# Two of four weight pieces on a second DMA queue, in a gated mix of linear attention and SwiGLU

## The chip, the cores and the metric

The kernel runs on one core of a Trainium2 chip. The metric is the device time of one execution in microseconds, as the median of several runs; lower is better.

## The reference

The input `x` has 2048 rows (tokens) of 512 values, in bfloat16. Two branches are computed from it and mixed per token. The inputs of branch B called `B_x` are not used; both branches read `A_x`.

```
g = sigmoid((x * gate_w).sum(-1, keepdims=True))
# branch A: linear attention, 32 heads of 16
q, k, v = split(x @ wqkv)
phi(t) = where(t > 0, t + 1, exp(t)) + 1e-6
kv = einsum("bhsd,bhse->bhde", phi(k), v);  z = phi(k).sum over s
a  = (einsum("bhqd,bhde->bhqe", phi(q), kv) / (phi(q) . z + 1e-6)) @ wo
# branch B: SwiGLU with F = 1376
b  = (silu(x @ w1) * (x @ w3)) @ w2
out = g * a + (1 - g) * b
```

## The kernel before

The 2048 tokens are handled in 16 tiles of 128 (`t`), or in 4 blocks of 512 (`tb`). The inner dimension of 512 is split into four chunks of 128 (`kc`). All weights stay in SBUF.

The projections to q and k come first. The weights for both lie in one tile, `wqk` (128 x 4 x 1024); chunk `kc` of it, called piece `kc` below (256 KB), is one load. A projection of one tile of tokens is four matmuls, one for each piece (L183), with the transposed tokens `xT` as the stationary operand. ScalarE (ACT) takes the exponential from PSUM, VectorE (DVE) makes `pk` or `pq` from it, GpSimd (POOL) adds up `pk` for z, and TensorE collects G = x^T phi(k) in four PSUM banks (L231). Then follow, per block, the SwiGLU matmuls (L303 and L309, ten of 128 columns of F each), a remainder of 96 columns together with the gate (L245), the small products that turn G into kv and M2, and the output matmuls (L475 for branch A, L492 for branch B with `w2`), which VectorE mixes (L498) and SyncE stores (L508).

The order of the work is written out by hand: the program runs under a manual schedule, each engine does its instructions in program order, and semaphores join them. Nearly all loads are issued by SyncE (SP, `dq`), in the order of the code. A DMA that SP issues uses one of eight semaphores in turn, and waits for the eighth DMA before it in that count, where that is not known to be over.

The beginning matters here. TensorE first does 13 matmuls on constants (L359). The first two tiles of tokens are loaded as they are (`xN`, L129, one load of 256 KB) and transposed on TensorE with an identity (L365); VectorE (L379, L381, L394) and ScalarE (L380, L382) copy the results to `xT`. The later tiles of `xT` come by transposing loads from SP (`load_xT`, L123), which stand behind the four pieces of `wqk` (`load_wqk`, L126) in SP's queue. The matmuls of the first two tiles are interleaved by piece: four matmuls with piece 0, the transposes for chunk 3, four matmuls with piece 1, and then k alone with pieces 2 and 3, before q with the same pieces:

```python
for kc in range(2):
    for n, t in (("k", 0), ("q", 0), ("k", 1), ("q", 1)):
        first_mm(n, t, kc)
    if kc == 0:
        transpose_kc(3, bank[0])
        nc.vector.tensor_copy(out=xT[:, 3, 0 : 2 * P], in_=bank[0][:, 0 : 2 * P])
for kc in range(2, KC):
    for t in range(2):
        first_mm("k", t, kc)
```

ScalarE begins with a one-column exponential into `act_pre`, a tile that nobody reads, which brings the load of its function table to the front (L130). On its own DMA queue it issues one load, `touch` (L133): 16 columns of pieces 1 to 3, 12 KB, which nobody reads either.

After the x loads SP issues the remainder columns (`wr`), `w1`, `w3`, `wv`, `wo`, `w2` (1.25 MB, one load, L154) and `w2x`.

Of the kernel before, what the change touches and what calls it, by code (L numbers as in the profile page):

```python
# [8 lines left out]
ACT = mybir.ActivationFunctionType  # L9
# [3 lines left out]
BF16 = mybir.dt.bfloat16  # L13
# [3 lines left out]
def kernel(  # L17
# [17 lines left out]
    nc = tc.nc  # L35
    P = nc.NUM_PARTITIONS

    Bb, S, D = A_x.shape
# [3 lines left out]
    KC = D // P  # L42
# [4 lines left out]
    FC = F // P  # L47
# [14 lines left out]
    wqkv_r = A_wqkv.rearrange("(kc d) n -> d kc n", d=P)  # L62
# [3 lines left out]
    consts = ctx.enter_context(tc.tile_pool(name="consts", bufs=1))  # L66
# [5 lines left out]
    warm = nc.const_aps.tensor(1.0, [P, 256], BF16)  # L72
# [7 lines left out]
        out=bmask[:], in_=bmask[:], pattern=[[-Dh, HPC], [0, Dh]], compare_op=ALU.is_ge,  # L80
# [3 lines left out]
        out=bmask[:], in_=bmask[:], pattern=[[Dh, HPC], [0, Dh]], compare_op=ALU.is_ge,  # L84
# [23 lines left out]
    wqk = consts.tile([P, KC, 2 * D], BF16, name="wqk")  # L108
# [6 lines left out]
    w3 = consts.tile([P, KC, F0], BF16, name="w3")  # L115
    w2 = consts.tile([P, FC, D], BF16, name="w2")
    xT = consts.tile([P, KC, S], BF16, name="xT")
    act_pre = consts.tile([P, 1], BF16, name="act_pre")
    dq = nc.sync

    def load_xT(t):
        ts = slice(t * P, (t + 1) * P)
        dq.dma_start(out=xT[:, :, ts], in_=x2d[ts, :], transpose=True)  # L123

    def load_wqk(kc):
        dq.dma_start(out=wqk[:, kc, :], in_=wqkv_r[:, kc, 0 : 2 * D])  # L126

    x_first = x2d[0 : 2 * P, :].rearrange("(p j) d -> p j d", j=2)
    dq.dma_start(out=xN[:, 0:2, :], in_=x_first)  # L129
    nc.scalar.activation(out=act_pre[:], in_=warm[:, 0:1], func=ACT.Exp)  # L130

    touch = consts.tile([P, KC - 1, 16], BF16, name="touch")
    nc.scalar.dma_start(out=touch[:], in_=wqkv_r[:, 1:KC, 0:16])  # L133
    for kc in range(KC):
        load_wqk(kc)
    natural = {3: (2, 4), 5: (4, 8), 8: (8, 16)}
    for t in range(2, NT):
        load_xT(t)
# [3 lines left out]
    with nc.allow_non_contiguous_dma(reason="gate column"):  # L142
        dq.dma_start(
            out=wr[:, :, 2 * FR : NR], in_=gate_w.rearrange("(kc d o) -> d kc o", d=P, o=1)
# [3 lines left out]
    for w, w_r, cuts in ((w1, w1_r, (0, KC)), (w3, w3_r, (0, KC))):  # L148
# [2 lines left out]
    dq.dma_start(out=wv[:], in_=wqkv_r[:, :, 2 * D : 3 * D])  # L151
    dq.dma_start(out=wo[:], in_=A_wo.rearrange("(kc d) n -> d kc n", d=P))
    w2_r = B_w2[0:F0, :].rearrange("(fc f) d -> f fc d", f=P)
    dq.dma_start(out=w2[:], in_=w2_r)  # L154
    w2x_r = B_w2[F0:F, :].rearrange("(i r) d -> i (r d)", i=RP)
    dq.dma_start(
        out=w2x[:].rearrange("p r d -> p (r d)"),
        in_=w2x_r[None].to_broadcast([TPB, RP, RG * D]),
# [442 lines left out]
```

## Time and profile before

| | us |
|---|---|
| median of 3 runs | 178.73 (178.44 to 178.74) |
| the profiled execution, its own time | 177.74 |
| its span in the profile | 176.0 |
| TensorE busy in the span | 171.3 |
| VectorE, ScalarE, GpSimd busy | 110.5, 59.1, 63.3 |

All times in the profile count from the start of the span. The granted clock of TensorE was 1.0 throughout. The profiled execution spends 1.70 us outside the span, and the median of the runs lies 0.99 us above the profiled execution. "PEld" is TensorE's loading of weights, which overlaps its matmuls; "SPq" and "ACTq" are the instructions with which SP and ACT issue DMAs. The landing of a DMA is counted from its issue to the completion of its semaphore.

### The profile page before, as it was taken

The numbers are of one execution on the slowest core, as the hardware profiler recorded it, in microseconds if no ns is written. First come the engines' busy times: TensorE is split into PE (matmuls) and PEld (weight loads), VectorE is DVE, ScalarE is ACT, GpSimd is POOL, SyncE is SP. The second block draws the span as 40 slices with busy tenths as digits, with TensorE's granted clock in tenths as the row PEclk, the third lists the DMA queues.
The fourth block names the chain that finished last, engine by engine and source line by source line (L and its number), as shares of the span: only waits on it lengthen the run. The fifth ranks groups of instructions, "written<-read, shape, count | busy, mean of one in ns | idle before, by whom it ended". The sixth has DMA issues, their size and how long they took to land.

```text
span 176.0 us, 2668 instructions
## 1 busy us (share of the span) xinstructions
PE 171.3 (97%) x952; PEld 82.4 (47%) x969; DVE 110.5 (63%) x207; ACT 59.1 (34%) x109; POOL 63.3 (36%) x106
## 2 busy tenths in 40 slices
PE   8999999999999999999999999999999999999993
PEld 5444444444456443444444466444444444444453
DVE  0399788888764899777343477853435775344363
ACT  4364544544753533322433101224226122422000
POOL 5087656656300668586300044540000662000000
DMA  5988969997205112323200013330000233000001
GB/s 172 277 197 207 164 123 237 403 352 231 78 4 56 22 30 41 78 63 91 58 0 0 0 34 84 84 89 0 0 4 0 60 89 89 4 0 0 30 30 60
DMA packets 29360, 15.58 MB, mean 88 GB/s; under 512 B 21156, under 2 KB 27556, under 8 KB 29348
## 3 DMA queue, kind: packets, MB, share of 16 engines
q1 hardware_dynamic: 28948, 15.41, 35.1%
q8 instruction: 7, 0.11, 0.3%
q10 hardware_dynamic: 400, 0.01, 0.1%
q14 instruction: 5, 0.04, 0.1%
HBM read 8.86 MB, written 2.10 MB: 62 GB/s over the span
## 4 chain that ended last, share of the span: by engine, by line
PE 95%; DMA 2%; issue 1%; SPq 0%; DVE 0%
PE bank L303 20%; PE bank L492 20%; PE bank L309 19%; PE bank L183 16%; PE bank L231 8%; PE bank L475 8%; PE bank L245 3%; DMA wqk<-in_A_wqkv_dram 2%; PE bank L278 2%; PE bank L447 0%; SPq L129 0%; PE bank L462 0%; DVE o L498 0%; PE bank L365 0%
## 5 line engine op out<-in xcount | busy, mean ns | idle before, releaser
L315 DVE TENSOR_TENSOR hT<-bank,sg 128x512 bf16<-128x512 f32 x40 | 27.3, 682 | 31.0 <-PE bank L309 28.9
L303 PE MATMUL bank<-xT,w 128*128 128x512 bf16 x158 | 40.8, 379 | 0.2
L309 PE MATMUL bank<-xT,w 128*128 128x512 bf16 x156 | 40.5, 379 | 0.2
L314 ACT ACTIVATE sg<-bank 128x512 bf16<-128x512 f32 x40 | 23.9, 597 | 45.9 <-PE bank L303 45.9
L492 PE MATMUL bank<-w,hT 128*128 128x512 bf16 (+2 forms) x176 | 37.0, 355 | 0.5 <-issue 0.3
L337 POOL TENSOR_TENSOR pqs<-pq,rden 128x512 bf16<-128x512 bf16 x16 | 16.9, 1057 | 54.3 <-issue 46.8
L183 PE MATMUL bank<-wqk,xT 128*128 128x512 bf16 x126 | 30.2, 379 | 0.1
L215 POOL TENSOR_TENSOR zacc<-zacc,pk 128x128 f32<-128x128 f32 x56 | 23.3, 447 | 10.4 <-DVE pk L201 10.4
L492 PEld LDWEIGHTS <-hT 128*128 128x128 bf16 x180 | 16.7, 98 | 18.4 <-issue 0.8
L309 PEld LDWEIGHTS <-w 128*128 128x128 bf16 x160 | 15.7, 98 | 18.9
L303 PEld LDWEIGHTS <-w 128*128 128x128 bf16 x160 | 15.5, 98 | 18.2 <-issue 0.2
L498 DVE SCALAR_TENSOR_TENSOR o<-bank,omg_all,aga 128x512 bf16<-128x512 f32 (+2 forms) x18 | 12.4, 692 | 14.5 <-PE bank L492 11.7
L183 PEld LDWEIGHTS <-xT 128*128 128x128 bf16 x128 | 12.5, 98 | 14.9 <-issue 0.3
L322 POOL TENSOR_TENSOR pr<-pq,zb 128x512 f32<-128x512 bf16 x16 | 18.4, 1155 | 0.1
L231 PE MATMUL bank<-pk,xN 128*128 128x512 bf16 x62 | 16.3, 379 | 0.2
L475 PE MATMUL bank<-M,pqT 128*128 128x512 bf16 x61 | 15.6, 379 | 0.1
L196 ACT ACTIVATE eq<-bank 128x512 bf16<-128x512 f32 x16 | 9.4, 597 | 16.0 <-PE bank L183 14.9
L201 DVE SCALAR_TENSOR_TENSOR pk<-bank,emk 128x512 bf16<-128x512 f32 x16 | 11.1, 692 | 1.6
L196 ACT ACTIVATE ek<-bank 128x512 bf16<-128x512 f32 x16 | 9.4, 597 | 6.5 <-PE bank L183 6.5
L201 DVE SCALAR_TENSOR_TENSOR pq<-bank,emq 128x512 bf16<-128x512 f32 x16 | 11.1, 692 | 0.5
L326 DVE TENSOR_REDUCE den<-pr 128x32 f32<-128x512 f32 x16 | 10.8, 676 | 0.0
L231 PEld LDWEIGHTS <-xN 128*128 128x128 bf16 x64 | 6.3, 98 | 7.5
(54 smaller groups left out, 95.6 us busy)
## 6 DMA issues: line engine op xcount, KB each, us to landing
w<-in_B_w_dram SPq DMA_DIRECT2D x3, 1280.0 KB, 10.3
out_dram<-o SPq DMA_DIRECT2D x15, 128.0 KB, 1.9
wqk<-in_A_wqkv_dram SPq DMA_DIRECT2D x4, 256.0 KB, 3.7
xN<-in_A_x_dram SPq DMA_DIRECT2D x1, 1024.0 KB
xN<-in_A_x_dram SPq DMA_DIRECT2D x2, 256.0 KB, 2.9
xN<-in_A_x_dram SPq DMA_DIRECT2D x1, 512.0 KB, 4.2
wv<-in_A_wqkv_dram SPq DMA_DIRECT2D x1, 512.0 KB, 11.2
wo<-in_A_wo_dram SPq DMA_DIRECT2D x1, 512.0 KB, 12.2
```

The costliest lines, as they stand in the source:

```text
L183: nc.tensor.matmul(ps[:], lhsT=xT[:, kc, t * P : (t + 1) * P], rhs=w[:, kc, :], start=(kc == 0), stop=(kc == KC - 1),)
L196: nc.scalar.activation(out=e[:], in_=ps[:], func=ACT.Exp)
L201: nc.vector.scalar_tensor_tensor(out=dst, in0=ps[:], scalar=0.0, in1=em[:], op0=ALU.max, op1=ALU.add)
L215: nc.gpsimd.tensor_tensor(out=(zaccb if t == NT - 1 else zacc)[:, cs], in0=zacc[:, cs], in1=pk[t][:, cs], op=ALU.add,)
L231: nc.tensor.matmul(bank[kc][:], lhsT=xN[:, t, kc * P : (kc + 1) * P], rhs=pk[t][:], start=(t == 0), stop=(t == NT - 1),)
L303: nc.tensor.matmul(g_ps[:], lhsT=w1[:, kc, fs], rhs=xT[:, kc, tok], start=(kc == 0), stop=(kc == KC - 1),)
L309: nc.tensor.matmul(u_ps[:], lhsT=w3[:, kc, fs], rhs=xT[:, kc, tok], start=(kc == 0), stop=(kc == KC - 1),)
L314: nc.scalar.activation(out=sg[:], in_=g_ps[:], func=ACT.Silu)
L315: nc.vector.tensor_tensor(out=hT[tb][:, fc, :], in0=u_ps[:], in1=sg[:], op=ALU.mult)
L322: nc.gpsimd.tensor_tensor(out=pr[t][:], in0=pq[:, t, :], in1=zb[:], op=ALU.mult)
L475: nc.tensor.matmul(ps[:], lhsT=pqT[:, c, ts], rhs=M2[:, c, :], start=(c == 0), stop=(c == KC - 1),)
L492: nc.tensor.matmul(ps[:, 0 : cs.stop - cs.start], lhsT=hT[tb][:, fc, tt * P : (tt + 1) * P], rhs=w2[:, fc, cs], start=(fc == 0 and not sta ...
```

## The change

Pieces 1 and 3 of `wqk` are issued by ScalarE instead of SP. The first exponential of ScalarE writes its one column into `wqk[:, 1, 0:1]` instead of `act_pre`, so that the load of piece 1, which overwrites that column, has to wait for it; the load of piece 3 follows on the same queue. The load `touch` is left out. The load of `w2` is split into two halves of five chunks each.

```diff
-    act_pre = consts.tile([P, 1], BF16, name="act_pre")
...
-    def load_wqk(kc):
-        dq.dma_start(out=wqk[:, kc, :], in_=wqkv_r[:, kc, 0 : 2 * D])
+    def load_wqk(kc, queue):
+        queue.dma_start(out=wqk[:, kc, :], in_=wqkv_r[:, kc, 0 : 2 * D])
...
-    nc.scalar.activation(out=act_pre[:], in_=warm[:, 0:1], func=ACT.Exp)
-
-    touch = consts.tile([P, KC - 1, 16], BF16, name="touch")
-    nc.scalar.dma_start(out=touch[:], in_=wqkv_r[:, 1:KC, 0:16])
+    nc.scalar.activation(out=wqk[:, 1, 0:1], in_=warm[:, 0:1], func=ACT.Exp)
+
     for kc in range(KC):
-        load_wqk(kc)
+        load_wqk(kc, nc.scalar if kc in (1, 3) else dq)
...
-    dq.dma_start(out=w2[:], in_=w2_r)
+    for a, b in ((0, FC // 2), (FC // 2, FC)):
+        dq.dma_start(out=w2[:, a:b, :], in_=w2_r[:, a:b, :])
```

## Prediction

> **What bounds the kernel now.** I read the page first (sections 1 and 4), then the chain of waits over the first 9 us, then the timeline of SP's queue, ACT and TensorE there, and last the DMA queues in short windows.
>
> Busy time of the engines and the chain that ended last, from the page:
>
> ```profile
> PE 171.3 (97%) x952; PEld 82.4 (47%) x969; DVE 110.5 (63%) x207; ACT 59.1 (34%) x109; POOL 63.3 (36%) x106
> PE 95%; DMA 2%; issue 1%; SPq 0%; DVE 0%
> ```
>
> TensorE is busy 171.3 of 176.0 us. It begins at 0.84 and the last 2 us are the final store, so some 2 us of idle time can be won anywhere, and the stretches after 9 us show hardly any. The edits all act on loads, so I look where a load still holds TensorE. The chain, first 9 us (start, length, what):
>
> ```profile
> 1.26 3.11 DMA wqk<-in_A_wqkv_dram
> 4.37 0.04 issue
> 4.41 1.02 PE bank L183 x4
> 5.43 0.11 PE bank L365 x2
> 5.54 3.60 PE bank L183 x16
> ```
>
> The first real matmul (L183) starts at 4.41 because piece 0 of wq and wk lands at 4.37. The timeline there (start, length, engine, line):
>
> ```profile
> 0.81 0.39 SPq L129 DMA_DIRECT2D xN<-in_A_x_dram  x1
> 0.86 0.43 ACTq L133 DMA_DIRECT2D touch<-in_A_wqkv_dram  x1
> 1.26 1.84 SPq L126 DMA_DIRECT2D wqk<-in_A_wqkv_dram  x4
> 2.10 0.20 ACT L130 ACTIVATE act_pre<-const-bfloat16-1.0 128x1 bf16<-128x1 bf16 x1
> 4.08 0.28 ACT L380 ACTIVATE xT<-bank 128x128 bf16<-128x128 f32 x1 [1.78 <-PE bank L365]
> 4.32 0.62 PEld L183 LDWEIGHTS <-xT 128*128 128x128 bf16 x4
> 6.83 0.53 PEld L183 LDWEIGHTS <-xT 128*128 128x128 bf16 x3 [0.27 <-issue]
> ```
>
> Two losses stand here. The weights of the first matmul load at 4.32 and it starts 0.09 later; the transposing matmuls (L365) start 0.01 after theirs, at 3.64 and 3.65. So at most 0.08 us hangs on piece 0. And the weight load at 6.83 follows 0.27 us of idleness. The matmul starts there are 6.03, 6.25, 6.46, 6.82, 7.04; the usual spacing is 0.86/4 = 0.216, so one start is 0.14 late, that of the first matmul on piece 3. Issue times and landings, asked piece by piece: piece 0 1.26 + 3.1 = 4.37, piece 1 1.72 + 3.4 = 5.12, piece 2 2.18 + 3.9 = 6.08, piece 3 2.67 + 4.1 = 6.77. TensorE wanted them at 4.33, 5.38, 6.25 and 6.68: piece 3 alone comes late, piece 0 just, and the two between have 0.26 and 0.17 to spare.
>
> The DMA queues (q1 is SP's, q10 ACT's), from 2.0 to 2.9 us, then from 2.9 to 3.3 us, then from 3.3 to 4.0 us; share of 16 engines in the last column:
>
> ```profile
> q1 hardware_dynamic: 105, 0.22, 79.2%
> ...
> q1 hardware_dynamic: 64, 0.10, 66.0%
> q10 hardware_dynamic: 400, 0.01, 56.2%
> ...
> q1 hardware_dynamic: 152, 0.28, 106.8%
> ```
>
> From 2.9 us on the DMA engines are full, so each piece lands when the bytes ahead of it are through. And the small unused load (touch) took its 400 packets all between 2.9 and 3.3: after nearly all of xN (105 packets before 2.9), ahead of piece 0, which SP had issued at 1.26. It cost 56.2% of 0.4 us = 0.22 us of every engine.
>
> **The change, part by part.**
>
> *No touch load.* Everything behind it comes 0.22 us sooner: piece 0 at 4.15, and with the order unchanged piece 1 at 4.90, piece 2 at 5.86, piece 3 at 6.55. Worth 0.08 us at the first matmul, which is then held by its weights. TensorE would want the others at 5.30, 6.17 and 6.60, so piece 3 no longer stalls it: 0.14 us more. Bounds: nothing, if what follows is delayed otherwise; and if xN too comes sooner (its 3.61 sets the transposes), up to 0.2 us more.
>
> *Pieces 1 and 3 on ACT's queue, held by the activation.* The activation does the same 128x1 work and ends at 2.30. Then ACT issues piece 1 and piece 3, 0.43 + 0.03 us each by the touch row: 2.36 to 2.79 and 2.82 to 3.25. Piece 1 goes out 0.64 later than before, piece 3 0.15 later, piece 2 (now second on SP) 0.46 earlier. Behind the waiting instruction on ACT stand only the copies of xT at L380 and L382; L380 starts at 4.08, so 0.83 us of cover is left. If the cover went, each further us would delay the third matmul by as much. No row shows a bulk load on ACT's queue, so its start is bounded: SP's xN was issued at 0.81 and its packets began about 1.92 (1.1 us); touch, the one ACT load, 0.86 and 2.9 (2.0 us). That makes piece 1 ready at 3.47 to 4.4, and piece 3 at 3.9 to 4.9. The last packets of piece 0 leave at about 3.55 to 3.8. I take the near end, because touch's later start is explained by xN having the engines until then. What follows hangs on whose turn it is: touch went ahead of a piece 0 that had been issued 1.6 us earlier, whole and in one go, when xN was through. So I expect piece 0, piece 1 (ACT), piece 2 (SP), piece 3 (ACT), the order of today, and no further cost. The other end is piece 1 behind piece 2, a rival below.
>
> The Trainium skill, "DMA: Bandwidth & Descriptors", section on queues, rings and completion order, says that each DMA engine goes round-robin between queue rows, a whole packet at a time, with some 9 to 17 descriptors in a typical one. The touch rows agree with that turn-taking; whether 2 KB rows keep whole pieces together no run here shows.
>
> *SP two issues shorter.* The transposed loads of xT start at 2.2 instead of 3.15. In the queue they lie behind the same bytes, and nobody waits for them: xT of tile 2 lands at 3.15 + 4.1 = 7.25 and its first matmul is at 8.12. Worth nothing. That they are generated beside ACT's two loads is the third rival.
>
> *w2 in two halves.* One issue of 3.66 us (L154, held back by full queues) becomes two, at most 0.5 us more of SP. SP is free from 36.9 (w2x issued) to 46.1 (the z transpose, for which it waits 9.1 us on POOL), and w2, landing at 43.8, is first read at 67.2. Cost 0; uncovered it would be 0.5. In number, the extra load takes touch's place among the loads that later issues count back to: each issue from z on waits for a load one later in order, none of which lands late (w1 at 33.9, wo at 40.2; zrow is issued at 49.3). Cost 0.
>
> **The sum.** 0.08 + 0.14 = 0.22 us off. The profiled execution took 177.74 us, 1.70 over its span, so 177.52; the median of the runs is 0.99 above it, and taking off the same 0.22 gives 178.5 us. TensorE is dense afterwards, so a shift of the projections moves the end by as much: k of tile 0 is ready for the G products 0.09 before they start (8.89, 8.98), and moves along.
>
> **Rivals.**
>
> *Piece 1 behind piece 2.* If ACT's queue starts by touch's 2.0 us, or the two queues share the engines row by row, pieces 1 and 2 both end where piece 2 would, at 5.86. TensorE waits from 5.30 to 5.86, then runs 4 matmuls (0.86) and 2 (0.43), and takes piece 3 at 7.15 instead of 6.82: +0.33 us, 179.1 us. It decides from the point where piece 1 is ready later than some 3.6. For it: the margin is only 0.1 us. Against it: touch's turn.
>
> The Trainium skill, same page, section on issuing engines, says that loads issued from several engines share the same 16 DMA engines, and only issue time is saved. By that the later issue of piece 1 buys nothing, and it would land with piece 2; the full engines after 2.9 agree.
>
> *ACT's issue held behind SP's transposes.* SP now starts issuing xT (1.30 and 1.26 us each) at 2.23, just before ACT's first issue at 2.36. If both draw on one generator in turn, piece 1 is generated after xT of tile 2, at 3.5, and piece 3 after tile 3, at 4.8. Then L380 waits until 5.2, piece 1 lands about 6.2, TensorE takes 1.29 us for its six matmuls and piece 3 at 7.5: +0.7 us, 179.4 us. Against it: touch's issue (0.43) ran beside xN's (0.39) unslowed; but those were plain loads.
>
> *xN sooner as well.* Touch overlaps xN's tail. If xN came 0.2 us sooner and all else with it: 0.42 off, 178.3 us. Against it: 105 of 128 packets of xN were through before touch began.
>
> **How the numbers follow.** Forecast 0.42, piece 1 late 0.30, held generator 0.16, xN sooner 0.12. A measurement of this kernel tells about 0.2% (0.36 us) from no change. The forecast at 0.22 off lies mostly within that (0.36, and 0.06 faster); the late piece at 0.33 on, with ends of 0.1 and 0.6, splits (0.13 same, 0.17 slower); the held generator is slower (0.16); xN sooner is mostly faster (0.10 and 0.02). Sums: faster 0.16, same 0.51, slower 0.33. The range runs from 178.2, below the last rival, to 179.4, the middle of the third; the forecast's own is 178.35 to 178.75.
>
> **What would show it.** Right: no ACT load of 400 small packets; piece 0's wait gone (first L183 about 0.01 after its weights); no idle weight load before piece 3; the first G product about 0.2 us before 8.98. The late piece: idle TensorE between the transposes of L365 and the fifth L183, some 0.5 us. The held generator: ACT's issues longer than 0.43 us, or L380 later than 4.08. Wrong altogether: a wait after 9 us that is not there now.

## The result, and the profile after

The changed kernel is slower. Its median is 180.19 us (6 runs, 179.60 to 182.39) against 178.58 us for the kernel before on the same chip (6 runs, 177.89 to 178.83); the ratio is 1.0102, 95% interval 1.0081 to 1.0124. The ratio leaves out the run of 182.39 us, in which the granted clock was 0.989 instead of 0.998 to 1.0. The profiled execution took 180.96 us, its span is 179.1 us (before: 177.74 and 176.0).

Busy time of the engines and the chain that ended last, from the page of the changed kernel:

```profile
PE 172.9 (97%) x969; PEld 82.6 (46%) x969; DVE 110.9 (62%) x207; ACT 59.2 (33%) x109; POOL 63.3 (35%) x106
PE 93%; DMA 4%; ACT 1%; ACTq 0%; DVE 0%; issue 0%
```

TensorE's share is unchanged, and the share of the DMAs in the chain has doubled. The chain from 2.1 to 12 us (start, length, what) says where. Line numbers have moved by one to three: L125 loads a piece, L122 an x tile, L181 is the projection, L363 the transposes on TensorE.

```profile
2.10 0.21 ACT wqk L129
2.31 0.02 issue
2.33 0.40 ACTq L125
2.73 0.03 issue
2.76 7.06 DMA wqk<-in_A_wqkv_dram
9.82 0.04 issue
9.86 2.32 PE bank L181 x10
```

The chain no longer runs through piece 0. It runs through ACT: the activation that holds, the issue of piece 1, and piece 3, which takes 7.06 us from its issue to 9.82. The timeline shows the issues and what TensorE did (idle time before in brackets):

```profile
1.25 0.89 SPq L125 DMA_DIRECT2D wqk<-in_A_wqkv_dram  x2
2.19 2.61 SPq L122 DMA_TRANSPOSE xT<-in_A_x_dram  x2
2.33 0.88 ACTq L125 DMA_DIRECT2D wqk<-in_A_wqkv_dram  x2
4.03 0.28 ACT L378 ACTIVATE xT<-bank 128x128 bf16<-128x128 f32 x1 [1.72 <-PE bank L363]
4.29 1.44 PE L181 MATMUL bank<-wqk,xT 128*128 128x512 bf16 x4
7.70 1.45 PE L181 MATMUL bank<-wqk,xT 128*128 128x512 bf16 x6 [1.86 <-DMA wqk<-in_A_wqkv_dram]
9.86 0.38 PE L181 MATMUL bank<-wqk,xT 128*128 128x512 bf16 x1 [0.71 <-DMA wqk<-in_A_wqkv_dram]
```

The first matmul starts at 4.29 instead of 4.41. Then TensorE waits 1.86 us for piece 1, runs six matmuls, and waits again for piece 3. The first matmul on piece 3 stands at 9.86; before it stood at 6.82. That is 3.04 us later, and the span is 179.1 - 176.0 = 3.1 us longer: this execution lost all of it before 10 us. The medians differ by less, 1.6 us; how long the two pieces take differs from execution to execution (piece 3 landed at 9.82 here, and at 9.19 when the same kernel was profiled again).

### The profile page after: what moved, and what is told of

Its sections match the earlier page's. It is cut to its first block, busy times and chain, and to the rows that moved or that the text cites. A ratio compares the mean times of both kernels' runs of the same rounds, so it can differ in the third digit from the quotient of the medians.

```text
span 179.1 us, 2685 instructions
## 1 busy us (share of the span) xinstructions
PE 172.9 (97%) x969; PEld 82.6 (46%) x969; DVE 110.9 (62%) x207; ACT 59.2 (33%) x109; POOL 63.3 (35%) x106
## 4 chain that ended last, share of the span: by engine, by line
PE 93%; DMA 4%; ACT 1%; ACTq 0%; DVE 0%; issue 0%
PE bank L490 19%; PE bank L301 19%; PE bank L307 19%; PE bank L181 14%; PE bank L229 8%; PE bank L473 8%; DMA wqk<-in_A_wqkv_dram 4%; PE bank L243 3%; PE bank L276 2%; ACT L129 1%; PE bank L445 0%; ACTq L125 0%; PE bank L460 0%; DVE o L496 0%; ACT wqk L129 0%
## 5 line engine op out<-in xcount | busy, mean ns | idle before, releaser
L301 PE MATMUL bank<-xT,w 128*128 128x512 bf16 x160 | 41.1, 379 | 0.0
L307 PE MATMUL bank<-xT,w 128*128 128x512 bf16 x160 | 41.1, 379 | 0.0
L490 PE MATMUL bank<-w,hT 128*128 128x512 bf16 (+2 forms) x180 | 37.5, 355 | 0.0
L181 PE MATMUL bank<-wqk,xT 128*128 128x512 bf16 x128 | 31.0, 383 | 2.6 <-DMA wqk<-in_A_wqkv_dram 2.6
L181 PEld LDWEIGHTS <-xT 128*128 128x128 bf16 x128 | 12.5, 98 | 17.9 <-issue 3.5
L473 PE MATMUL bank<-M,pqT 128*128 128x512 bf16 x64 | 16.1, 379 | 0.0
L196 DVE TENSOR_SCALAR emk<-ek 128x512 bf16<-128x512 bf16 x16 | 7.3, 459 | 4.6 <-ACT ek L194 4.6
```

Of the source, the lines that this page charges most:

```text
L181: nc.tensor.matmul(ps[:], lhsT=xT[:, kc, t * P : (t + 1) * P], rhs=w[:, kc, :], start=(kc == 0), stop=(kc == KC - 1),)
L301: nc.tensor.matmul(g_ps[:], lhsT=w1[:, kc, fs], rhs=xT[:, kc, tok], start=(kc == 0), stop=(kc == KC - 1),)
L307: nc.tensor.matmul(u_ps[:], lhsT=w3[:, kc, fs], rhs=xT[:, kc, tok], start=(kc == 0), stop=(kc == KC - 1),)
L473: nc.tensor.matmul(ps[:], lhsT=pqT[:, c, ts], rhs=M2[:, c, :], start=(c == 0), stop=(c == KC - 1),)
L490: nc.tensor.matmul(ps[:, 0 : cs.stop - cs.start], lhsT=hT[tb][:, fc, tt * P : (tt + 1) * P], rhs=w2[:, fc, cs], start=(fc == 0 and not sta ...
```

## The experiments

The table collects what follows: landing of the four pieces in each profiled execution (us from the span's start, good to 0.1 us), the start of the first matmul on piece 3, and the ratio of times to the kernel before with its interval. The first matmul on piece 3 depends on more than the landings: TensorE begins at half its pace, and the moment at which the pace doubles differs between profiles, as shown further down.

| kernel | 0 | 1 | 2 | 3 | matmul on 3 | ratio to before |
|---|---|---|---|---|---|---|
| before | 4.37 | 5.12 | 6.08 | 6.77 | 6.82 | 1 |
| changed | 4.25 | 7.66 | 5.0 | 9.82 | 9.86 | 1.0102 (1.0081 to 1.0124) |
| changed, profiled again | 4.2 | 7.0 | 5.3 | 9.19 | 9.23 | 1.0138 (1.0105 to 1.0172) |
| all pieces on SP | 4.4 | 5.4 | 6.4 | 7.13 | 7.17 | 1.0013 (0.9994 to 1.0031) |
| no hold | 5.51 | 4.5 | 6.6 | 5.9 | 9.77 | 1.0101 (1.0038 to 1.0165) |
| no hold, more warm-up | 5.65 | 4.8 | 6.9 | 6.1 | 8.74 | 1.0054 (1.0038 to 1.0071) |
| x loads plain | 4.25 | 6.84 | 6.6 | 7.6 | 8.18 | 1.0083 (1.0046 to 1.0119) |
| x loads plain, run again | 4.15 | 6.9 | 6.7 | 8.41 | 8.46 | 1.0069 (1.0047 to 1.0092) |
| x loads held back | 4.25 | 6.3 | 5.1 | 6.9 | 7.62 | 1.0177 (1.0147 to 1.0208) |
| only piece 3 on ACT | 4.2 | 6.72 | 7.6 | 7.7 | 8.07 | 1.0052 (1.0018 to 1.0086) |
| one queue, that order | 4.2 | 7.0 | 5.7 | 9.02 | 9.06 | 1.0115 (1.0074 to 1.0156) |
| touch kept | 4.45 | 6.8 | 5.1 | 9.01 | 9.05 | 1.0089 (1.006 to 1.0118) |
| before, w2 in halves | 4.4 | 5.0 | 5.9 | 6.7 | 7.80 | 1.0018 (1.0004 to 1.0032) |

Two theories were set against each other. Theory 1: SP's transposed x loads, now issued 0.9 us sooner, run beside ACT's plain loads on the same DMA engines, and the transposing stalls those. Theory 2: ACT's queue is merely late, and then shares the engines with whatever SP has queued.

**All pieces back on SP.**

```diff
-    nc.scalar.activation(out=wqk[:, 1, 0:1], in_=warm[:, 0:1], func=ACT.Exp)
+    act_pre = consts.tile([P, 1], BF16, name="act_pre")
+    nc.scalar.activation(out=act_pre[:], in_=warm[:, 0:1], func=ACT.Exp)
...
-        load_wqk(kc, nc.scalar if kc in (1, 3) else dq)
+        load_wqk(kc, dq)
```

> Undone: all four pieces back on SP, the first activation writes its own tile again; still without the small unused load and with w2 in halves. If ACT's queue is the cause (both theories below), pieces 1 and 3 land at about 4.9 and 6.6 us and the time is that of before or up to 0.3 us less, 178.3 to 178.6. If the missing small load or the halves of w2 cost the time, it stays near 180.2.

The median was 178.64 us against 178.34 us of before, ratio 1.0013. The loss is gone, so ACT's queue carries it. But nothing was won either: without the small load, pieces 1 to 3 landed 0.3 to 0.4 us later than before, not 0.2 sooner.

**The hold taken away.**

```diff
-    nc.scalar.activation(out=wqk[:, 1, 0:1], in_=warm[:, 0:1], func=ACT.Exp)
+    act_pre = consts.tile([P, 1], BF16, name="act_pre")
+    nc.scalar.activation(out=act_pre[:], in_=warm[:, 0:1], func=ACT.Exp)
```

> The hold alone taken away: ACT issues pieces 1 and 3 from about 0.86 us. Theory 1 (SP's transposed loads beside ACT's plain loads stall both): the pieces are through, all but the end of piece 3, before the first transposed packet at about 5 us, so they land by 5 and 7 us and the time is 178.3 to 179.0; piece 0 may come 0.5 us later, since ACT takes its turn. Theory 2 (ACT's queue is just late, and shares the engines with whatever SP has queued): the same 178.3 to 179.0, if the lateness was the hold; if ACT's queue starts late by itself, piece 1 lands at 6 us or later and the time is 179.5 to 180.2.

A miss: three of four runs took 180.85 to 180.88 us, one 178.85. Pieces 1 and 3 were early, as expected, and cost xN and piece 0 their time. The DMA queues from 2.6 to 3.6 us of this kernel (packets, MB, share of 16 engines):

```profile
q1 hardware_dynamic: 96, 0.19, 49.9%
q10 hardware_dynamic: 66, 0.14, 43.9%
```

ACT's 2 KB packets run mixed with those of xN, 66 beside 96 in the same microsecond. They do not wait until xN is through. TensorE began on x only at 4.29 and got piece 0 at 5.51, and its timeline shows a second loss (L182 is the projection in this kernel, L364 the transposes):

```profile
5.56 1.86 PE L182 MATMUL bank<-wqk,xT 128*128 128x512 bf16 x4 [0.44 <-DMA wqk<-in_A_wqkv_dram]
7.22 0.42 PE L364 MATMUL bank<-ident,xN 128*128 128x128 bf16 x2
7.43 2.93 PE L182 MATMUL bank<-wqk,xT 128*128 128x512 bf16 x8
```

Four matmuls in 1.86 us are some 0.43 us apart; before, four of them took 1.02. The spacing falls to 0.216 only at about 9.5 us. TensorE stood idle for 0.5 us before x and again before piece 0, and kept half its pace for long.

**No hold, but 22 warm-up matmuls.**

```diff
-    warm_step(13)
+    warm_step(22)
```

> The kernel without the hold, with 22 instead of 13 matmuls on constants ahead of the first transposes, so that TensorE does not stand idle while x comes. If TensorE's half pace until 9.4 us was the larger part of that kernel's 180.86 (three of four runs; the fourth 178.85), it now runs at full pace from the first matmul on piece 0 at 5.5 us or soon after, and nearly all runs take 178.6 to 179.3. If the late loads were the cause, it stays at 180.5 to 181.

All ten runs lay between 178.75 and 179.81 us. The median, 179.23, is in the expected range, but five of the ten runs are above it. Full pace came a little later than expected too, about 0.6 us into the matmuls on piece 0, which began at 6.19. The median is 1.6 us below that of the kernel without the longer warm-up, although the warm-up itself holds the first transposes back to 5.5 us. So the half pace was the larger part of the loss in the three slower of the four runs without the hold. (The ratios, 1.0101 and 1.0054, count the fourth run as well, and differ by 0.8 us.) The Trainium skill, "TensorE: Matmul & The Clock Gate", part 1, says that the clock goes to full after a busy window of about 3.4 us, and that this window runs freely, so that the same kernel warms up at different moments. The profiles agree that the moment moves: full pace was reached by 3.8 us with all pieces on SP, by 4.4 before, near 6.8 with the longer warm-up and near 9.5 without it; of the changed kernel, after 5.1 in one profile and by 4.3 in the other. The length of the window they do not show: with all pieces on SP, full pace came 2.9 us after the first matmul, which is less than 3.4. The granted clock of the profiled executions was 0.998 to 1.0 throughout and does not show the change; the spacing does.

**The x loads plain, in runs of 256 B.**

```diff
+        if t < 8:
+            dq.dma_start(out=xT[:, :, ts], in_=x2d[ts, :].rearrange("p (kc c) -> p kc c", c=P))
+            return
         dq.dma_start(out=xT[:, :, ts], in_=x2d[ts, :], transpose=True)
```

> The changed kernel, with the transposed loads of the x tiles 2 to 7 replaced by plain loads of the same bytes in runs of 256 B (these tiles of xT then hold x untransposed, so the rows of these tokens are not the reference's). Theory 1 (the transposing is what stalls ACT's loads): piece 1 lands at 5.5 to 6 us and piece 3 by 7.2, the time falls to 178.6 to 179.2. Theory 2 (sharing with any bytes that SP has queued, in small packets): pieces 1 and 3 land late as in the changed kernel, about 7.7 and 9.8 us, and the time stays at 180 or so.

The median was 179.37 us. Piece 3 landed at 7.6 instead of 9.82, and piece 1 only 0.8 us sooner, at 6.84, which is later than theory 1 had it. Piece 2, on SP, came 1.6 us later than in the changed kernel; why is not shown. The ratio is only 0.0019 (0.34 us) below that of the changed kernel and the intervals overlap, so both were run once more on one chip.

> The changed kernel unaltered, for a second look beside the next run. If the stall of piece 3 by SP's transposed loads is the rule and not an accident of one execution, its 128 packets again hold the engines for 1.3 us each or more (2.1 in the first look; 0.7 where nothing transposed ran beside them), and it lands at 8.5 to 10 us. If it was an accident, it lands by 7.5.

> The changed kernel with plain loads for the x tiles 2 to 7 once more (these tiles of xT hold x untransposed), on the same chip as the changed kernel. Theory 1 (transposed loads stall ACT's): pieces 1 and 3 land by 7 and 7.7 us, and the median is 0.5 to 1.5 us below that of the changed kernel. Theory 2 (any bytes beside them): the two medians agree within 0.3 us.

The changed kernel's piece 3 landed at 9.19, so the stall was no accident of one execution. With plain loads piece 1 landed at 6.9, as theory 1 had it, but piece 3 only at 8.41, later than its 7.7. The medians of before, changed and plain were 178.18, 180.41 and 179.51 us. So 0.90 us of the 2.23 us go with the transposing and 1.33 us stay. The size is rough: the first pair of runs puts less on the transposing. Each theory holds a part. The DMA queues while piece 3 was loaded show the transposing part: first the changed kernel from 5.7 to 9.2 us, then the same kernel profiled again from 5.6 to 8.6 us, then the plain loads run again from 5.65 to 8.0 us, and last, for comparison, the kernel of the next experiment from 5.35 to 6.6 us, where nothing of SP ran beside ACT's.

```profile
q10 hardware_dynamic: 138, 0.25, 53.0%
q1 hardware_dynamic: 658, 0.16, 44.6%
```

```profile
q1 hardware_dynamic: 865, 0.21, 71.1%
q10 hardware_dynamic: 149, 0.26, 46.5%
```

```profile
q1 hardware_dynamic: 1295, 0.47, 76.5%
q10 hardware_dynamic: 146, 0.25, 30.8%
```

```profile
q10 hardware_dynamic: 143, 0.25, 52.1%
```

ACT moved the same 0.25 to 0.26 MB in all four. Its packets took 0.53 x 3.5 = 1.86 us and 0.465 x 3.0 = 1.40 us per engine beside transposed packets, 0.308 x 2.35 = 0.72 us beside plain ones, while SP moved twice to three times as much, and 0.521 x 1.25 = 0.65 us alone. The same bytes took about twice the time, or more, beside the transposed loads. Not all of it need be work: in the changed kernel's second profile the shares of the two queues add up to 118%, so packets of both were under way at once, and a part may be waiting. But the bytes show the loss as well: both queues together moved 0.41 MB in 3.5 us and 0.47 MB in 3.0 us with transposed loads, and 0.72 MB in 2.35 us with plain ones. (SP issues a plain load in some 0.6 us and a transposed one in 1.3, so the plain kernels had more of SP's bytes beside ACT's, not fewer.)

**The x loads held back until piece 3 has landed.**

```diff
+    hold = consts.tile([P, 16], BF16, name="hold")
+    dq.dma_start(out=hold[:], in_=wqk[:, 3, 0:16])
     natural = {3: (2, 4), 5: (4, 8), 8: (8, 16)}
```

> The changed kernel, with SP's transposed loads held back until piece 3 has landed (SP issues a load of 16 columns out of piece 3 into a spare tile ahead of them). Both theories: with SP's queue empty piece 1 lands at 5.4 to 5.8 us and piece 3 at 6.2 to 6.6, which shows what ACT's queue does alone; then the x tiles come late, xT of tile 2 at about 9.5 instead of 8.1 where it is wanted, so 1 to 2 us are lost there and the time is 179.5 to 180.5. If the pieces land late even so (7 us and more), ACT's queue is slow by itself and both theories fall.

The time was 181.55 us, 1 us more than the upper end, since x tile 2 now comes at 10.24. What counts is the pieces: with no x loads of SP beside them, piece 1 landed at 6.3, later than the 5.4 to 5.8 expected, and piece 3 at 6.9. TensorE waited for piece 1:

```profile
6.33 2.75 PE L183 MATMUL bank<-wqk,xT 128*128 128x512 bf16 x12 [0.71 <-DMA wqk<-in_A_wqkv_dram]
```

The queues of this kernel from 3.9 to 4.25 us, then from 4.25 to 4.4 us:

```profile
q1 hardware_dynamic: 66, 0.13, 97.7%
...
q10 hardware_dynamic: 9, 0.02, 81.2%
q1 hardware_dynamic: 28, 0.03, 63.5%
```

ACT's first packet comes after 4.25 us, though its load was issued at 2.33: at least 1.9 us. It did so in the changed kernel too, in both plain kernels and with touch kept. By then piece 2 is nearly through. The row of matmuls above holds four on piece 1 and two on piece 2 before the first on piece 3, which starts at 6.33 + 6 x 0.215 = 7.62. So late pieces on ACT's queue, without SP's x loads, cost 7.62 - 6.82 = 0.80 us in this execution. The rest of the changed kernel's delay, 3.04 - 0.80 = 2.24 us in its first profile and 2.41 - 0.80 = 1.61 us in its second, came with SP's x loads beside them. Whether ACT's queue is late by itself, or behind the load that SP had issued just before, is open: in every run SP had issued a load some 0.6 us or less ahead of ACT's.

**The small load kept on ACT's queue.**

```diff
+    touch = consts.tile([P, KC - 1, 16], BF16, name="touch")
+    nc.scalar.dma_start(out=touch[:], in_=wqkv_r[:, 1:KC, 0:16])
```

> The changed kernel with the small unused load put back at the front of ACT's queue. If ACT's queue was slow to start (1.9 us from issue to first packet) because piece 1 was its first load, piece 1 now starts 1.1 us after its issue, at 3.4 to 3.6 us, goes beside piece 0 and 2 and lands by 5.7, before the transposed loads: time 178.4 to 179.3. If the start is always that late, piece 1 starts at 4.2 again and the time is that of the changed kernel, 180.

The median was 179.87 us, and ACT's first packet of piece 1 came after 4.25 us again. So the late start is not only that of a queue's first load.

**Only piece 3 on ACT.**

```diff
-    nc.scalar.activation(out=wqk[:, 1, 0:1], in_=warm[:, 0:1], func=ACT.Exp)
+    nc.scalar.activation(out=wqk[:, 3, 0:1], in_=warm[:, 0:1], func=ACT.Exp)
...
-        load_wqk(kc, nc.scalar if kc in (1, 3) else dq)
+        load_wqk(kc, nc.scalar if kc == 3 else dq)
```

> The changed kernel with piece 1 back on SP: SP issues pieces 0, 1 and 2, ACT only piece 3, held by the activation (which now writes into piece 3). If sharing the engines with SP's transposed loads is the large part, piece 3, issued at 2.33 us, starts at about 4.2 beside the end of piece 2, meets the first transposed load and lands at 7 to 9 us instead of 6.77: time 178.6 to 180.3, less than the changed kernel since only one piece meets them. If the large part was piece 1 alone (TensorE's first long wait), the time is 178.3 to 178.7.

The time was 179.33 us, by the ratio about half the loss, in the range of the first reading. But the profile does not bear out that reading's path: piece 1, on SP, itself landed at 6.72, 1.6 us later than before, and from 3.8 to 4.2 us, before ACT's first packet, its queue kept the engines busy for half the time only. Why is open.

**One queue, in about the order of the changed kernel's bytes.**

```diff
-    nc.scalar.activation(out=wqk[:, 1, 0:1], in_=warm[:, 0:1], func=ACT.Exp)
-
-    for kc in range(KC):
-        load_wqk(kc, nc.scalar if kc in (1, 3) else dq)
+    act_pre = consts.tile([P, 1], BF16, name="act_pre")
+    nc.scalar.activation(out=act_pre[:], in_=warm[:, 0:1], func=ACT.Exp)
+
+    load_wqk(0, dq)
+    load_wqk(2, dq)
+    load_xT(2)
+    load_wqk(1, dq)
+    load_xT(3)
+    load_wqk(3, dq)
...
-        load_xT(t)
+        if t > 3:
+            load_xT(t)
```

> No second queue, but about the order in which the changed kernel's bytes went: SP issues piece 0, piece 2, x tile 2 (transposed), piece 1, x tile 3 (transposed), piece 3. If two queues working at once on transposed and plain loads cause the stall (theory 1), one queue in this order lands piece 1 at about 6.5 and piece 3 at 7.5 to 8 us, and the loss is 0.8 to 1.3 us at most (179.1 to 179.7), less than the changed kernel's. If any plain load near a transposed one stalls, whatever the queue, piece 3 lands at 9 us or later and the time is 180.2 or more.

The median was 180.1 us, above the range for theory 1, so this kernel did not tell the theories apart. SP needs 1.2 to 1.3 us to issue a transposed load, so that piece 3 was issued only at 5.39. It landed 3.6 us after that, no slower than a piece before. What it shows is that pieces behind transposed loads are late on one queue too.

**w2 in halves alone.**

> The kernel of before with w2 in two halves and nothing else. Expected within 0.2 us of before (no wait of TensorE on w2, SP idle after it). If the halves cost something by the count of loads that SP's issues wait for, 0.3 us or more.

178.66 us against 178.18, ratio 1.0018. By the ratio that is 0.3 us, with an interval from 0.07 to 0.57 us, and by the medians 0.5 us: a little more than expected. The profiled execution shows no wait for w2; it ran the first five matmuls at half pace (first matmul on piece 3 at 7.80 although the piece had landed at 6.7), as those of several kernels above did their first four. Whether the halves cost anything is not settled.

No version beat the kernel before: the best, with all pieces on SP, only equalled it.

## Why the prediction was wrong

**The step that failed first** is the choice of the near end for ACT's queue. The prediction bounded the time from issue to first packet by 1.1 us (SP's xN) and 2.0 us (touch), and took 1.1, explaining touch's lateness by xN having the engines. The measured time was the far end, 1.9 to 2.0 us, and 1.6 at the least in the kernel without the hold, where ACT's packets did not wait for xN but ran mixed with its own. The row of the same queue was there, and the row of the other queue was preferred. That made the order "piece 0, 1, 2, 3" wrong.

The reading that touch went "whole and in one go" ahead of piece 0 failed with it, and on the lines that the prediction shows: from 2.9 to 3.3 us SP's queue moved 0.10 MB beside touch, some 48 packets of 2 KB, and at most 128 - 105 = 23 of them can have been of xN. The other 25 or more were of piece 0, so touch and piece 0 ran side by side. Nothing there spoke for whole pieces taking turns.

**The first rival had the right mechanism, but not the size.** Piece 1 behind piece 2 was priced at 0.33 us, with piece 1 ready at 5.86. With SP's x loads out of the way it landed at 6.3 and the first matmul on piece 3 came 0.80 us later than before. The rule of the Trainium skill named there, that loads from several engines share the same DMA engines, spoke against the change and held.

**The term that was missing** is SP's transposed loads. The prediction gave the shorter list of SP issues a worth of nothing, because they lie behind the same bytes in the queue and nobody waits for xT. Nobody did. But being issued at 2.19 instead of 3.15, and no longer behind pieces 1 and 3 in one queue, they came onto the engines beside these pieces. The two medians on one chip put 0.90 us on the transposing, and 1.33 us on the late start and the sharing together; the first pair of runs puts less on the transposing (0.34 us by the ratios). No case in the prediction had this, and the range ended at 179.4.

**Touch.** The term of 0.22 us was not won. Piece 0 came 0.12 us sooner and the first matmul started 0.12 sooner, but with all pieces on SP the other pieces came later than before and the time did not fall (1.0013). With touch and w2 in halves they came as before (5.0, 5.9 and 6.7). Either the load does something for pieces 1 to 3, or landings differ by that much from one execution to the next; no run separates these.

**The signs.** The prediction named a new wait after 9 us as the sign of being wrong altogether, and it came: 0.71 us for piece 3, up to 9.86. After 10 us no wait of TensorE is new.

**Right:** ACT's issues took 0.88 us for two, and L378 began at 4.03, so the copies of xT lost nothing. The held generator fell too: with SP's transposed loads held back, ACT's first packet came no sooner. w2 is not waited for.

## What to carry to other kernels

A second DMA queue added no DMA engines here: the packets of both shared the same 16. Moving a load to it takes away the order that one queue gave, so ask which transfers behind it will now run beside it, transposed ones above all. And take a queue's start time from a row of that same queue, even if the row is a small one.

## What the runs showed of the hardware

- ACT's queue brought its first packet 1.6 to 2.0 us after the issue (touch in the kernel before: 2.0), SP's queue that of xN 1.0 to 1.4 us after.
- Packets of 2 KB from two queues run mixed: 96 and 66 in one microsecond.
- The packets of a plain load of 256 KB took 0.65 us per DMA engine alone, 0.72 us beside plain packets of 256 B, and 1.4 to 1.9 us beside transposed ones.
- TensorE's pace doubled at moments between 3.8 and 9.5 us of the span; nine more warm-up matmuls, in a kernel where it had stood idle for half a microsecond twice, took 1.6 us off the median.
